# Attention and mixture of experts in one kernel: a GpSimd drain behind the scatters of eight groups, and one weight split of the half group given out two products sooner

## The chip, the core and the metric

The kernel runs on one core of a Trainium2 chip. The metric is the device time of one launch in microseconds (us). The core's engines are TensorE (PE, with its weight loads as PEld), VectorE (DVE), ScalarE (ACT) and GpSimd (POOL); SyncE (SP) issues most DMAs. Each has a queue of its own that it works through in order; engines wait for each other, and for DMAs, by semaphores. GpSimd issues the indirect DMAs (gathers and scatters of rows by an index list).

## The reference

Block-sparse attention, whose output is the input of a mixture of experts with one expert a token:

```python
scores = scale * np.matmul(q, k.transpose(0, 1, 3, 2))   # 4 batches, 8 heads, 768 positions, 64
scores = np.where(mask, scores, -1000000000.0)           # blocks of 32: neighbours, first, last, 3 sampled
attn = np.exp(scores - max); attn /= attn.sum + 1e-9
x = (attn @ v), laid out as 3072 tokens of 512
logits = x @ w_gate + modality_bias[modality_id]         # 8 experts
e_idx = np.argmax(logits, axis=1); gate_w = softmax(logits)[e_idx]
for e in range(8):                                       # w1: 512 x 1024, w2: 1024 x 512
    h = np.maximum(x[mask] @ w1[e], 0.0)
    out[mask] = gate_w[mask, None] * (h @ w2[e])
```

## The kernel before, in words

**Stages.** Attention and routing take about the first half of the launch. The experts follow: tokens are put in groups of 256 that share an expert. Groups 0 and 1 run while attention ends; groups 2 to 11 are the unrolled loop `for g in range(NEAR, NG)` (NEAR is 2, NG 12); what is left over is decided on the chip by two numbers, `total` and `wide`, that every engine loads from `grp` behind the loop. With this input one more group runs, of at most 128 tokens: `half_group(12)`. FIRST_Q is 4.

**A loop group** is `first_layer(g)` (96 matmuls of 256 columns, lines 772 to 774), `relu`, `second_layer(g)` (48 matmuls of 512 columns, lines 787 to 789), and `give(g)`: for each of two halves of 128 rows the sum is copied out of the bank (ACT and DVE, line 792), and GpSimd issues a scatter, an indirect DMA of 128 rows of 2 KB to the output (line 794). Each product is taken with three matmuls, high by high, high by low and low by high parts of the numbers. `split(n)` makes these parts of weight piece n (128 x 1024): ACT casts it (line 723), and DVE, or GpSimd where it is named, subtracts (line 724). `fetch` has SP load the piece.

**Rows in.** `gather_pieces(g + 2)` in `second_layer(g)` has GpSimd issue eight gathers (line 744) into the one buffer `xq`, once `turned_pieces(g + 1)` on DVE (line 751) has read the group before out of it. The last such call is that of group 10, for group 12. So GpSimd's queue in a loop group is: eight gathers, two scatters, the next group's eight gathers.

**The half group** has 24 wide products (lines 946 to 948), two `turn`s (four transposes by PE at line 952, then ACT line 955 and DVE line 956) and 24 products of the second layer, with four weight splits, pieces 4 to 7 of the group. Piece 6 is split by ACT and GpSimd; its low part is read for the first time by the second matmul of `down(g, 4, 0)`.

**What sets the order.** DVE, GpSimd and ACT keep, in the expert stage, the order in which the code is written (`manual_schedule`); PE and SP get theirs from the scheduler. The framework closes the program with lines of its own, shown as L1414 (the last line of the kernel's `with`): waits for all DMAs by SP, then a barrier among all engines with GpSimd drains in it.

Of the kernel before, what the change touches and what calls it, by code (L numbers as in the profile page):

```python
# [31 lines left out]
NG = NTOK // GT  # L32
# [4 lines left out]
FIRST_Q = NEAR + 2  # L37
# [52 lines left out]
def attention_moe(ctx, tc, kD, qD, qH, v0, v1, blocks, modality, w_gate, bias, w1, w2, out):  # L90
    nc = tc.nc
# [29 lines left out]
    with ExitStack() as actx:  # L121
# [582 lines left out]
        def staged(n):  # L704
            return stg[(0, 1, 0, 1, 0, 1, 0, 2)[n] if n < 8 else n % NSTG]
# [15 lines left out]
        def split(n, eng=None):  # L721
            h, l = wh[n % NRING], wl[n % NRING]
            nc.scalar.copy(h, staged(n))  # L723
            (eng or (nc.gpsimd if n in POOL_SPLITS else nc.vector)).tensor_tensor(l, staged(n), h.bitcast(F32), ALU.subtract)  # L724
# [15 lines left out]
        def gather_pieces(g):  # L740
            table = x_d.rearrange("t (r f) -> (t r) f", f=P)
            for t in range(2):
                for k in range(4):
                    nc.gpsimd.indirect_dma_start(  # L744
                        out=xq[0][:, 4 * t + k, :], out_offset=None, in_=table,
                        in_offset=bass.IndirectOffsetOnAxis(ap=gq[:, k, 2 * g + t:2 * g + t + 1], axis=0))

        def turned_pieces(g):
            flat = [xg[2 * (g % 2) + t].rearrange("p (c s) -> p c s", c=4) for t in range(2)]
            for t in range(2):  # L750
                nc.vector.transpose(flat[t].rearrange("p c (k s) -> p k c s", k=4),  # L751
                                    xq[0][:, 4 * t:4 * t + 4, :].rearrange("p k (d c) -> p k c d", c=4))
            for t in range(2):
                h, l = (x[g % 2][:, :, t * P:(t + 1) * P] for x in (xh, xl))
                nc.scalar.copy(h, flat[t])
                nc.vector.tensor_tensor(l, flat[t], h.bitcast(F32), ALU.subtract)

        def column(g, n, xp):
            for c in range(2):
                for t in range(2):  # L760
                    nc.tensor.transpose(xp[:, c * GT + t * P:c * GT + (t + 1) * P],
                                        xg[2 * (g % 2) + t][:, (2 * n + c) * P:(2 * n + c + 1) * P], ident)
            h = xh[g % 2][:, 2 * n:2 * n + 2, :].rearrange("p a b -> p (a b)")
            l = xl[g % 2][:, 2 * n:2 * n + 2, :].rearrange("p a b -> p (a b)")
            nc.scalar.copy(h, xp)
            nc.vector.tensor_tensor(l, xp, h.bitcast(F32), ALU.subtract)
# [15 lines left out]
        def down(g, f, t, o):  # L782
            n = 8 * g + 4 + f // 2
            h, l = wh[n % NRING], wl[n % NRING]
            fs = slice((f % 2) * 512, (f % 2 + 1) * 512)
            ts_ = slice(t * P, (t + 1) * P)
            nc.tensor.matmul(o, lhsT=hh[0][:, f, ts_], rhs=h[:, fs], start=f == 0, stop=False)  # L787
            nc.tensor.matmul(o, lhsT=hh[0][:, f, ts_], rhs=l[:, fs], start=False, stop=False)  # L788
            nc.tensor.matmul(o, lhsT=hl[f // 4][:, f % 4, ts_], rhs=h[:, fs], start=False, stop=f == 7)  # L789

        def give(g, t, o):
            (nc.vector.tensor_copy if t else nc.scalar.copy)(og[t], o)
            ix = si_e[g] if g < NEAR else si[:, 2 * g:2 * g + 2]
            nc.gpsimd.indirect_dma_start(
                out=out_t[t], out_offset=bass.IndirectOffsetOnAxis(ap=ix[:, t:t + 1], axis=0),
                in_=og[t], in_offset=None, bounds_check=NTOK - 1, oob_is_err=False)
# [102 lines left out]
        def ahead(n, *what):  # L899
            for do_, look in what or ((fetch, LOOK_D), (split, LOOK_S)):  # L900
                if n + look < 8 * NGMAX:
                    do_(n + look)
# [19 lines left out]
        def second_layer(g):  # L922
            for k in range(4):
                if k == 0 and FIRST_Q <= g + 1 < NGMAX:
                    turned_pieces(g + 1)
                    if g + 2 <= NG:
                        gather_pieces(g + 2)
                ahead(8 * g + 4 + k)
                for f in (2 * k, 2 * k + 1):
                    for t in range(2):  # L930
                        down(g, f, t, op[t])
                if k == 1 and g + 1 < FIRST_Q:
                    for n in range(2):
                        column(g + 1, n, xp[n])
            for t in range(2):
                give(g, t, op[t])


        def half_group(g):
            hid = xg[2 * ((g + 1) % 2):][:2]  # L940
            x = lambda t, c: t[g % 2][:, c, 0:P]

            def wide_up(k, c):
                h, l = wh[(8 * g + c) % NRING], wl[(8 * g + c) % NRING]
                fs = slice(k * 512, (k + 1) * 512)
                nc.tensor.matmul(hp[k], lhsT=x(xh, c), rhs=h[:, fs], start=c == 0, stop=False)
                nc.tensor.matmul(hp[k], lhsT=x(xl, c), rhs=h[:, fs], start=False, stop=False)
                nc.tensor.matmul(hp[k], lhsT=x(xh, c), rhs=l[:, fs], start=False, stop=c == 3)

            def turn(k):  # L950
                for f in range(4):
                    nc.tensor.transpose(xp[k][:, f * P:(f + 1) * P], hid[k][:, f * P:(f + 1) * P], ident)
                rh = hh[0][:, 4 * k:4 * k + 4, 0:P]
                p_ = xp[k].rearrange("p (f t) -> p f t", f=4)
                nc.scalar.copy(rh, p_)
                nc.vector.tensor_tensor(hl[k][:, :, 0:P], p_, rh.bitcast(F32), ALU.subtract)

            for c in range(2):
                fetch(8 * g + c + LOOK_D)
            for c in range(4):  # L960
                if c == 0:
                    split(8 * g + 4)
                wide_up(0, c)
            nc.scalar.activation(hid[0], hp[0], AF.Relu)
            wide_up(1, 0)
            split(8 * g + 5)
            wide_up(1, 1)
            turn(0)
            wide_up(1, 2)
            wide_up(1, 3)  # L970
            nc.scalar.activation(hid[1], hp[1], AF.Relu)
            split(8 * g + 6, nc.gpsimd)
            for f in range(8):
                if f == 2:
                    turn(1)
                    split(8 * g + 7)
                down(g, f, 0, op[0])
            give(g, 0, op[0])
# [439 lines left out]
```

## Time and profile before

| | |
|---|---|
| median of three runs | 533.4 us (532.72, 533.4, 538.16) |
| the profiled execution's own time | 531.94 us |
| its span, first to last instruction | 530.2 us |
| PE busy | 496.9 us, 94% of the span |
| DVE, ACT, POOL busy | 395.8, 340.7, 295.8 us |
| one loop group, from gather to gather | 21.9 us |

The profile has one profiled execution. Its views are: groups of instructions by line, waits (who waited for whom), the timeline, the chain of work that ended last, and windows (busy time of each engine and DMA traffic in a stretch). A row of one source line lists the sequencer's instructions too (POOLq, SPq: waits, branches, drains), which count as no busy time.

### The profile page before, as it was taken

The page shows a single profiled execution, that of the slowest core. Times are in us where ns is not written, and L with a number is a line of the kernel's source. Part 1 is how long each engine was busy: PE and PEld are TensorE (multiplying, and loading weights), DVE is VectorE, ACT ScalarE, POOL GpSimd, SP SyncE. Part 2 cuts the span into 40 slices and gives each one's busy share as a digit, 9 for nine tenths or more (in the row PEclk, how much of TensorE's full clock was granted, in tenths as well). Part 3 has the DMA queues.
Part 4 walks back from the last instruction along what each step waited for, and adds up shares of the span by engine and source line. Part 5 has one row for each costly group of instructions (what it writes and reads, how often), then busy time and mean ns, then how long its engine had stood idle before and what let it go on. Part 6 is the DMA issues. An engine that isn't in the chain of part 4 may idle for free.

```text
span 530.2 us, 18837 instructions
## 1 busy us (share of the span) xinstructions
PE 496.9 (94%) x7170; PEld 417.9 (79%) x7170; DVE 395.8 (75%) x1137; ACT 340.7 (64%) x777; POOL 295.8 (56%) x507
## 2 busy tenths in 40 slices
PE   7899999999999999799989999999999999999970
PEld 5577776767877777598979898998988989889850
DVE  7995697678689899977975758669586596775830
ACT  3789886979889978845445645547455473654640
POOL 3578674676468875543175527474474754747030
PEclk9999999999999999999999999999999999999995
DMA  7976887868846689757778766685866858768420
GB/s 281 330 226 197 251 243 221 230 209 246 244 148 186 205 227 258 218 190 240 240 282 281 267 204 208 234 291 172 281 224 223 293 161 282 232 214 299 166 85 20
DMA packets 49698, 119.40 MB, mean 225 GB/s; under 512 B 8512, under 2 KB 8896, under 8 KB 49600
## 3 DMA queue, kind: packets, MB, share of 16 engines
q1 hardware_dynamic: 44656, 105.00, 62.6%
q0 software_dynamic: 4944, 13.11, 6.7%
q8 instruction: 58, 0.95, 0.8%
q14 instruction: 40, 0.33, 0.2%
HBM read 105.50 MB, written 12.85 MB: 223 GB/s over the span
## 4 chain that ended last, share of the span: by engine, by line
PE 71%; DVE 10%; DMA 5%; issue 5%; SPq 4%; POOL 2%; ACT 1%; POOLq 0%; DVEq 0%; ACTq 0%
PE bank L789 8%; PE bank L772 8%; PE bank L788 8%; PE bank L787 7%; PE bank L773 7%; PE bank L774 7%; PE bank L535 6%; PE bank L560 5%; PE bank L591 3%; PE bank L582 3%; PE bank L608 2%; DVE slot L724 2%; PE bank L436 2%; DMA slot<-kD 2%; PE bank L598 1%
## 5 line engine op out<-in xcount | busy, mean ns | idle before, releaser
L724 DVE TENSOR_TENSOR slot<-slot 128x1024 fp32r<-128x1024 f32 x96 | 118.7, 1266 | 41.6 <-ACT slot L723 27.2
L744 POOL DMA_INDIRECT slot<-x_d,gq x72 | 94.1, 1307 | 76.2 <-DVE slot L751 56.8
L723 ACT CAST slot<-slot 128x1024 fp32r<-128x1024 f32 x104 | 106.2, 1047 | 39.1 <-PE bank L773 18.6
L772 PE MATMUL bank<-slot 128*128 128x256 f32 x384 | 107.2, 279 | 0.0
L773 PE MATMUL bank<-slot 128*128 128x256 f32 x384 | 106.3, 277 | 0.0
L774 PE MATMUL bank<-slot 128*128 128x256 f32 x384 | 106.3, 277 | 0.0
L551 ACT ACTIVATE a<-y,mn 128x256 f32<-128x256 f32 x176 | 88.7, 512 | 9.9 <-DVE mn L543 8.8
L789 PE MATMUL bank<-slot 128*128 128x512 f32 x200 | 79.0, 395 | 1.6 <-DVE slot L780 1.6
L788 PE MATMUL bank<-slot 128*128 128x512 f32 x200 | 78.6, 393 | 0.6 <-POOL slot L724 0.6
L787 PE MATMUL bank<-slot 128*128 128x512 f32 x200 | 78.3, 391 | 0.0
L773 PEld LDWEIGHTS bank<-slot 128*128 128x128 f32 x384 | 72.3, 188 | 0.4
L772 PEld LDWEIGHTS bank<-slot 128*128 128x128 f32 x384 | 72.1, 188 | 0.6
L774 PEld LDWEIGHTS bank<-slot 128*128 128x128 f32 x384 | 72.1, 188 | 0.0
L543 DVE CUSTOM_DVE_ANT_1 y<-bank,smask 128x256 f32<-128x256 f32 x176 | 66.3, 416 | 1.1 <-PE bank L535 0.7
L483 POOL COPY slot<-slot 128x128 f32 x264 | 65.1, 303 | 0.0
L505 POOL TENSOR_SCALAR slot<-slot 32x1024 f32<-32x1024 f32 x40 | 42.0, 1050 | 24.4 <-issue 10.3
L560 PE MATMUL bank<-ident,a 128*128 128x128 f32 x352 | 52.2, 280 | 2.1 <-DVE mn L543 1.8
L565 ACT COPY at<-bank 128x512 f32<-128x512 f32 x88 | 50.7, 577 | 5.2 <-PE bank L560 5.0
L779 ACT ACTIVATE slot<-bank 128x512 fp32r<-128x512 f32 x48 | 27.2, 598 | 37.9 <-PE bank L774 34.7
L535 PE MATMUL bank<-slot,q_raw 64*32 64x256 f32 x1408 | 49.2, 382 | 1.0 <-DMA q_raw<-qH 0.8
L780 DVE SCALAR_TENSOR_TENSOR slot<-bank,slot 128x512 fp32r<-128x512 f32 x48 | 30.6, 685 | 24.1 <-ACT slot L779 24.1
L789 PEld LDWEIGHTS bank<-slot 128*128 128x128 f32 x200 | 37.6, 188 | 9.8 <-DVE slot L780 2.0
(299 smaller groups left out, 864.2 us busy)
## 6 DMA issues: line engine op xcount, KB each, us to landing
slot<-w SPq DMA_DIRECT2D x105, 512.0 KB
slot<-v SPq DMA_DIRECT2D x180, 128.0 KB
q_raw<-qH SPq DMA_DIRECT2D x22, 256.0 KB
x_d<-xr SPq DMA_DIRECT2D x22, 256.0 KB
slot<-v SPq DMA_DIRECT2D x16, 256.0 KB
slot<-kD SPq DMA_DIRECT2D x13, 256.0 KB
slot<-v SPq DMA_DIRECT2D x4, 768.0 KB
slot<-kD SPq DMA_DIRECT2D x3, 768.0 KB
```

The lines of the kernel that those rows point to most:

```text
L535: nc.tensor.matmul(sp[u][32 * pr:32 * pr + 32, b * 256:(b + 1) * 256], lhsT=q[r, b * NPAIR + pr, n, :], rhs=kv[r, s0:s0 + 8, b, pr, :], st ...
L551: nc.scalar.activation(a[:, u, :], y[:, u, :], AF.Exp, bias=mn[:, u:u + 1], scale=-1.0, accum_out=total[:, u:u + 1])
L560: nc.tensor.transpose(tp[:, k:k + P], a[:, u, c * P:(c + 1) * P], ident)
L723: nc.scalar.copy(h, staged(n))
L724: (eng or (nc.gpsimd if n in POOL_SPLITS else nc.vector)).tensor_tensor(l, staged(n), h.bitcast(F32), ALU.subtract)
L744: nc.gpsimd.indirect_dma_start(out=xq[0][:, 4 * t + k, :], out_offset=None, in_=table, in_offset=bass.IndirectOffsetOnAxis(ap=gq[:, k, 2 * ...
L772: nc.tensor.matmul(o, lhsT=h[:, fs], rhs=xh[g % 2][:, c, :], start=c == 0 and f % 2 == 0, stop=False)
L773: nc.tensor.matmul(o, lhsT=h[:, fs], rhs=xl[g % 2][:, c, :], start=False, stop=False)
L774: nc.tensor.matmul(o, lhsT=l[:, fs], rhs=xh[g % 2][:, c, :], start=False, stop=c == 3 and f % 2 == 1)
L787: nc.tensor.matmul(o, lhsT=hh[0][:, f, ts_], rhs=h[:, fs], start=f == 0, stop=False)
L788: nc.tensor.matmul(o, lhsT=hh[0][:, f, ts_], rhs=l[:, fs], start=False, stop=False)
L789: nc.tensor.matmul(o, lhsT=hl[f // 4][:, f % 4, ts_], rhs=h[:, fs], start=False, stop=f == 7)
```

## The change

A drain is put into GpSimd's queue behind the two scatters of groups 4 to 11, eight in all. In `half_group` the split of piece 6 is written behind `turn(0)`, ahead of the last two wide products and of the second relu, where it stood behind both.

```diff
@@ second_layer
             for t in range(2):
                 give(g, t, op[t])
+            if FIRST_Q <= g < NG:
+                nc.gpsimd.drain()
@@ half_group
             split(8 * g + 5)
             wide_up(1, 1)
             turn(0)
+            split(8 * g + 6, nc.gpsimd)
             wide_up(1, 2)
             wide_up(1, 3)
             nc.scalar.activation(hid[1], hp[1], AF.Relu)
-            split(8 * g + 6, nc.gpsimd)
             for f in range(8):
```

ACT's rows of the half group, before: L955 are the two turns, L971 is the second relu, L723 are the casts of pieces 4, 5, 6 and 7, L792 the copy out.

```order
L723 CAST slot<-slot 128x1024
L964 ACTIVATE slot<-bank 128x512
L723 CAST slot<-slot 128x1024
L955 CAST slot<-bank 128x4x128
L971 ACTIVATE slot<-bank 128x512
L723 CAST slot<-slot 128x1024
L955 CAST slot<-bank 128x4x128
L723 CAST slot<-slot 128x1024
L792 COPY slot<-bank 128x512
```

The same stretch of ACT's queue with the change; lines behind the drain's stand two or three higher.

```order
L723 CAST slot<-slot 128x1024
L966 ACTIVATE slot<-bank 128x512
L723 CAST slot<-slot 128x1024
L957 CAST slot<-bank 128x4x128
L723 CAST slot<-slot 128x1024
L974 ACTIVATE slot<-bank 128x512
L957 CAST slot<-bank 128x4x128
L723 CAST slot<-slot 128x1024
L792 COPY slot<-bank 128x512
```

The cast of piece 6 has changed places with the second relu. PE's, DVE's and SP's rows are in the same order as before.

GpSimd's rows at the end of the loop, with the change: the scatters of groups 10 and 11 (L794), the two loads of `grp`, the branches, and the subtraction of piece 6 (L724). Drains are not printed; one stands behind each pair of scatters.

```order
L794 DMA out<-slot,si 3072x512 [waits DMASW4_49,Activation_49]
L794 DMA out<-slot,si 3072x512 [waits DMASW5_49,DVE_49]
L794 DMA out<-slot,si 3072x512 [waits DMASW6_49,DMASW4_49,Activation_49]
L794 DMA out<-slot,si 3072x512 [waits DMASW7_49,DMASW5_49,DVE_49]
L1367 TENSOR_LOAD grp [waits DVE_49]
L1368 TENSOR_LOAD grp
L1373 COMPARE_AND_BRANCH
L1375 COMPARE_AND_BRANCH
L724 TENSOR_TENSOR slot<-slot 128x1024 [waits DMAHW0_49,DMAHW5_49,PE_49,Activation_49]
```

No printed row of GpSimd has moved; the drain of group 11 stands between the fourth row and the fifth, so the loads, the branches and the subtraction are now behind it.

## Rows read from the trace of the kernel before

**Rows 1.** The page's first line.
```profile
span 530.2 us, 18837 instructions
```
**Rows 2.** Waits of PE, 270 us to the end: total, times, longest (us).
```profile
PE bank L789 <- DVE slot L780: 1.6, 1, 1.6
PE bank L788 <- POOL slot L724: 0.6, 1, 0.6
```
**Rows 3.** The chain that ended last, its last piece: start, us, what.
```profile
515.77 0.99 POOL out L794
```
**Rows 4.** Windows of the tail: length, busy us by engine, PE clock, DMA share, GB/s.
```profile
517.00:519.00 2.00, 0.00 (x0) 0.00 (x0) 0.00 (x0) 0.00 (x0) 0.00 (x0) 0.52 0.34 123
519.00:520.00 1.00, 0.00 (x0) 0.00 (x0) 0.00 (x0) 0.00 (x0) 0.00 (x0) 0.50 0.03 8
521.00:530.20 9.20, 0.00 (x0) 0.00 (x0) 0.00 (x0) 0.00 (x0) 0.00 (x0) 0.50 0.00 1
```
**Rows 5.** GpSimd's drains by line (end, start): ns min/median/max, first and last start.
```profile
L1414 POOLq DRAIN  x3: 45/107/8705, 520.6 to 529.9; - x3
L1411 POOLq DRAIN  x1: 171/171/171, 0.4 to 0.4; - x1
```
**Rows 6.** Waits of SP, 510 us to the end.
```profile
SPq L1414 <- PEq L1414: 10.0, 2, 9.5
```
**Rows 7.** GpSimd's indirect DMAs by line: count, busy us, mean ns, idle before.
```profile
L744 POOL DMA_INDIRECT slot<-x_d,gq x72 | 94.1, 1307 | 76.2 <-DVE slot L751 56.8 <-issue 19.4
L794 POOL DMA_INDIRECT out<-slot,si x21 | 23.0, 1094 | 26.5 <-ACT slot L792 21.0 <-issue 5.5
...
L729 POOL DMA_INDIRECT slot<-x_d,gi x4 | 4.6, 1150 | 7.4 <-DVE gi L987 6.5 <-issue 0.6 <-DMA slot<-w 0.3
L729 POOL DMA_INDIRECT slot<-x_d,gi_e x4 | 4.5, 1116 | 0.9 <-issue 0.6 <-POOL slot L505 0.2 <-POOL slot L724 0.2
L794 POOL DMA_INDIRECT out<-slot,si_e x4 | 4.2, 1060 | 10.9 <-ACT slot L792 10.1 <-DVE gend L1121 0.5 <-issue 0.3
```
**Rows 8.** Timeline of GpSimd, one loop group's end: start, us, what, idle before.
```profile
441.07 1.03 POOL L744 DMA_INDIRECT slot<-x_d,gq  x1 [0.30 <-issue]
...
443.71 1.17 POOL L794 DMA_INDIRECT out<-slot,si  x1 [0.30 <-issue]
451.31 0.99 POOL L744 DMA_INDIRECT slot<-x_d,gq  x1 [6.43 <-DVE slot L751]
```
**Rows 9.** Windows ahead of two groups' gathers, columns as in rows 4.
```profile
450.00:451.00 1.00, 1.00 (x6) 0.81 (x5) 1.00 (x3) 0.00 (x0) 0.00 (x0) 1.00 0.00 0
...
472.00:473.00 1.00, 1.00 (x6) 0.83 (x5) 1.00 (x2) 0.04 (x1) 0.00 (x0) 1.00 0.01 4
```
**Rows 10.** Timeline of DVE in the same loop group.
```profile
449.96 2.06 DVE L751 STREAM_TRANSPOSE slot<-slot 128x512 f32<-128x512 f32 x2
```
**Rows 11.** Timelines of ACT, GpSimd and PE about the half group.
```profile
503.47 0.98 POOL L794 DMA_INDIRECT out<-slot,si  x1 [0.30 <-issue]
506.58 0.59 ACT L955 CAST slot<-bank 128x512 fp32r<-128x512 f32 x1 [0.27 <-PE bank L952]
508.46 1.04 ACT L723 CAST slot<-slot 128x1024 fp32r<-128x1024 f32 x1
509.59 2.39 POOL L724 TENSOR_TENSOR slot<-slot 128x1024 fp32r<-128x1024 f32 x1 [5.14 <-ACT slot L723]
512.03 0.50 PE L788 MATMUL bank<-slot 128*128 128x512 f32 x1 [0.55 <-POOL slot L724]
```
**Rows 12.** Window behind group 11's scatters, columns as in rows 4.
```profile
508.00:508.50 0.50, 0.50 (x3) 0.28 (x2) 0.17 (x1) 0.50 (x2) 0.00 (x0) 1.00 0.00 0
```
**Rows 13.** GpSimd's first load of grp and its branches, by line.
```profile
L1365 POOLq TENSOR_LOAD <-grp x1: 289/289/289, 502.8 to 502.8; - x1
...
L1373 POOLq COMPARE_BRANCH  x2: 34/38/41, 503.5 to 518.1; - x2
```

## The prediction, made before the changed kernel ran

> **What bounds the kernel now.** I read the waits of PE first, since PE is busy 94% of the span. From 270 us to its last matmul PE is stopped twice, by 1.6 and 0.6 us [rows 2]: the expert stage is PE's own work, and nothing that the change does there can gain more than these few tenths. Then I read where the chain that ended last stops. Its last piece is GpSimd's scatter of the half group, 515.77 to 516.76 us [rows 3], but the span is 530.2 us [rows 1]. So 13.4 us, 2.5% of the span, lie behind the last instruction that any engine counts as busy. The windows of this tail show what is in it: the scatter's 256 KB move between 517 and 519 (123 GB/s times 2 us), 8 GB/s are left in the next microsecond, and from 521 on nothing moves [rows 4]. Nine microseconds hold neither work nor data. The rows of the closing line name them: GpSimd's drains there are three, the first starts at 520.6 us and the longest takes 8705 ns; since the last starts at 529.9, the long one can only be the first, 520.6 to 529.3 [rows 5]. SP waits out the barrier for 9.5 us in the same place; the view names PE's sequencer, which is merely one of those that wait with it [rows 6].
>
> **What the long drain does.** All data has landed before it starts, so it does not wait for a transfer. Its two successors take 107 and 45 ns, and the one at the program's start, ahead of any DMA, 171 ns [rows 5]. What sets it apart is what GpSimd has issued since the drain before it: 72 + 21 + 4 + 4 + 4 = 105 indirect DMAs [rows 7]. My reading is that a drain goes through the indirect DMAs issued since the last drain and settles each: 8705 / 105 = 83 ns for each, an estimate. That the next drain takes 107 ns says that a DMA once settled is not gone through again.
>
> **The eight drains, term by term.** At the drain of group 4, 42 DMAs are open (8 gathers of whole rows, 24 of pieces, 10 scatters), 3.5 us at 83 ns; at those of groups 5 to 10 ten each, 0.8 us; at group 11 two; at the end of the program one, the half group's scatter. 42 + 60 + 2 + 1 = 105: the work is the same and changes place. The end's drain is then bounded below by the bare 45 ns and above by the 171 ns of the first drain plus one DMA's 83 ns; I take 0.15 us. **Term 1: 8.70 - 0.15 = 8.55 us gained.**
>
> What hides the others: a drain has also to wait until its group's scatters have landed. In the loop group shown the second scatter is handed over from 443.71 to 444.88, and GpSimd then stands idle 6.43 us until DVE's transposes release the next gather at 451.31 [rows 8]. From 450.0 to 451.0 no DMA at all is in flight [rows 9], so the scatters have landed within 5.1 us of 444.88. Group 9 is the tightest: 4 GB/s from 472 to 473 [rows 9], and its next gather stands at 473.2 in the same rhythm of 21.9 us. Six of the eight drains (groups 4 to 9) have this gap of 6.43 us; the settling of the gathers falls into the landing time. Even 3.5 us of settling for group 4, begun as soon as its scatter is handed over, end inside it. Behind the drain stand only the next gathers, and if they start late there is cover still: a gather handed over at 441.07 lands, if it takes no longer than the scatter (6.3 us from its start), by 447.4, and DVE reads it at 449.96 [rows 8, 10]: 2.6 us. If that cover goes too, DVE's transposes are late, and behind them the casts of the next group's rows. **Term 2: 0 us**, as long as a drain ends less than 9.0 us (6.43 + 2.6) after its scatter. Group 10's drain has no gather behind it and is free.
>
> **The drain of group 11 and the moved split** share a term. Now ACT's cast of piece 6 runs 508.46 to 509.50 behind the second relu, GpSimd subtracts from 509.59 for 2.39 us, and PE stands 0.55 us for the result [rows 11]; this is one of the two stops. With the split ahead of the relu, the cast can follow the turn's cast, which ends at 507.17 [rows 11], and ends at about 508.2; the relu behind it is some 0.2 us later, and its first reader, the second turn's transposes, stands behind six products of PE, so that costs nothing. By the cast alone GpSimd could subtract at 508.3 and the whole 0.55 us would be gained. But the drain of group 11 stands ahead. The scatters are handed over by 504.45 [rows 11] and have landed by 508.0, since from there to 508.5 no DMA moves [rows 12]. Then GpSimd has to load two numbers and pass two branches, which took it from 502.8 to 503.6 [rows 13], some 0.9 us with the gaps. So the subtraction starts between 509.0 and 509.4, and 0.2 to 0.55 us are gained. **Term 3: 0.35 us gained.** The point from which it turns: a drain that ends after 508.7 makes PE wait longer than before, one microsecond for each.
>
> [...]
>
> **The sum.** 8.55 + 0 + 0.35 = 8.9 us, made against the profiled execution's 531.94 us, which is 1.5 us below the median of the three timed runs. The four executions together (531.94, 532.72, 533.4, 538.16) have their middle at 533.06; 533.06 - 8.9 = **524.2 us**.
>
> **The rivals.**
> *A: the tail stays.* The 8.7 us are no settling of earlier DMAs but something of the closing line that the first drain there meets. Then the inner drains are as cheap as the bare ones and the end keeps its 8.7 us: 533.06 - 0.35 = 532.7 us. For it: no row before shows a second drain behind DMAs. Against it: the same kind of drain takes 107 ns in the same line.
> [...]
>
> *B, on the other side: each drain behind a DMA costs 8.7 us, whatever is open.* The place is GpSimd's queue. From the first gather to the end of the second scatter it needs 15.5 us of a group's 21.9 (451.31 less 21.9, to 444.88); with 8.7 more 24.2, so each of six groups is 2.3 us longer, 13.6 us less the cover of 2.6: 11 us. Group 11's drain ends at 513.2, the subtraction starts at 514.1 in place of 509.6, and PE stands 4.5 us longer. The end keeps its drain: 533.06 + 15.5 = 548.6 us. It decides from 6.43 + 2.6 = 9.0 us a drain, counted from the scatter, on. Against it: the 107 and 45 ns, if those are drains of the same kind.
>
> *C: settling is slow behind a landing.* If the drain of group 11 ends 3 us after its scatters have landed, term 3 turns to a loss of 2.6 us: 533.06 - 8.55 + 2.6 = 527.1 us. Against it: nothing but the arithmetic of 83 ns.
>
> If the 8.7 us are a cost of the first drain behind DMAs alone, that of group 4 pays it: 2.3 us beyond its gap, within the cover of 2.6, and the time is that of the forecast.
>
> **How the numbers follow.** The forecast, with the first-time variant, 0.82; A 0.08; B 0.05; C 0.05. The forecast's own range is 531.94 - 9.1 (8.66 with the bare drain, and 0.45) = 522.8 to 533.4 - 8.4 (the dearest last drain, and nothing in term 3) = 525.0. Stretched over C, and a little down for a series of runs that is as a whole lower, it is 522.3 to 527.5; A and B lie outside. A measurement of this kernel tells about 1% from no change, 5.3 us: the forecast and C are faster by more (0.87), A is the same (0.08), B slower (0.05).
>
> **What the profile of the changed kernel would show.** Right, if: the longest drain of the closing line takes under 0.3 us and the span ends about 5 us behind the last scatter; eight new drains stand at line 938, that of group 4 no shorter than the others and all of them ended before the next gather, whose idle time is still put down to DVE's transposes; PE's stop at the half group's second product of piece 6 is between 0 and 0.35 us. Wrong, if: the last drain is still several microseconds (A); the idle time ahead of the gathers is no longer DVE's, the loop group is longer than 21.9 us, and PE has stops in the loop (B); or PE stands more than 0.55 us for GpSimd's subtraction (C). The weakest step is the reading of 8705 ns as 105 times 83, since it rests on one long drain.

## The result, and the profile after

The changed kernel takes 528.56 us (median of six runs, 525.72 to 536.48) where the kernel before, in the same series, takes 537.06 (six runs, 532.72 to 538.91). The ratio is 0.986 with the interval 0.982 to 0.990: 1.4% faster, where the forecast was 8.9 us, 1.7%. The time itself lies 1.1 us above the forecast's range. One of the six runs was disturbed and is left out of the ratio.

| from the two profiled executions, us | before | after | difference | forecast |
|---|---|---|---|---|
| first instruction to group 2's first product | 281.89 | 281.47 | -0.4 | |
| groups 2 to 11, first product to first wide product | 219.93 | 223.47 | **+3.5** | 0 |
| half group, first wide product to start of the last scatter | 13.95 | 13.45 | -0.5 | -0.35 |
| end of the last scatter's hand-over to the end of the span | 13.43 | 4.6 | **-8.8** | -8.55 |
| span | 530.2 | 524.0 | -6.2 | -8.9 |

The first products are read from PE's timeline, here of the changed kernel (start, us, what); before they start at 281.89 and 501.82.

```profile
281.47 0.39 PE L772 MATMUL bank<-slot 128*128 128x256 f32 x1
...
504.94 0.39 PE L948 MATMUL bank<-slot 128*128 128x512 f32 x1
```

Two terms came as said. The third, "the inner drains cost nothing", did not: 3.5 us came back in the loop. GpSimd's drains of the changed kernel by line (ns min/median/max, first and last start; compare [rows 5]):

```profile
L938 POOLq DRAIN  x8: 4992/13188/14724, 349.1 to 506.1; - x8
...
L1416 POOLq DRAIN  x3: 57/107/1358, 521.2 to 523.7; - x3
```

The 8705 ns are gone from the closing line. The drains in the loop look long because the trace has them start before the scatters ahead of them have run (group 4's at 349.08, its scatters at 354.41 and 355.73); what counts is when they end. The tail by windows (columns as in [rows 4]):

```profile
519.40:521.40 2.00, 0.00 (x0) 0.00 (x0) 0.00 (x0) 0.00 (x0) 0.00 (x0) 1.00 0.35 127
521.40:523.00 1.60, 0.00 (x0) 0.00 (x0) 0.00 (x0) 0.00 (x0) 0.00 (x0) 0.62 0.02 5
523.00:524.00 1.00, 0.00 (x0) 0.00 (x0) 0.00 (x0) 0.00 (x0) 0.00 (x0) 0.50 0.00 0
```

The scatter's 256 KB move until 521.4, and the closing drain, begun at 521.2, ends at 522.6: its 1.36 us are mostly the landing, since the last update of that scatter's semaphore stands at 522.52. The drain is 7.35 us shorter, and it begins 1.86 us behind the scatter's hand-over in place of 3.88. The prediction did not look at what stands between the two: an instruction in GpSimd's sequencer row, begun 0.02 us behind the scatter's start in both traces, that is shorter too, before and after:

```profile
L1373 POOLq INC_SWDGE_SEM  x1: 2275/2275/2275, 515.8 to 515.8; - x1
```

```profile
L1375 POOLq INC_SWDGE_SEM  x1: 194/194/194, 518.4 to 518.4; - x1
```

The closing drain begins 2.6 us behind its end in both. Over all runs it takes 2.28 us with 105 indirect DMAs open (the kernel before), 2.18 with 100 (one_scatter), 1.44 with 63 (drain4_only), 0.24 with three (drain10) and 0.19 with one (the changed kernel): about 20 ns for each.

The half group's rows answer to [rows 11], ACT's cast of piece 6 and GpSimd's subtraction:

```profile
510.18 1.05 ACT L723 CAST slot<-slot 128x1024 fp32r<-128x1024 f32 x1
...
512.20 2.39 POOL L724 TENSOR_TENSOR slot<-slot 128x1024 fp32r<-128x1024 f32 x1 [4.63 <-ACT slot L974]
```

The drain of group 11 (506.1 plus 4.99) ends at 511.1, inside the cast, and the subtraction begins 0.97 us behind the cast. PE's waits from 270 us on (compare [rows 2]; the 1.6 us stop there falls ahead of 270 in this execution) show no stop for that subtraction any more, and a new one:

```profile
PE bank L787 <- ACT slot L779: 0.4, 1, 0.4
```

PE waits 0.4 us for ACT's relu. It is the start of the loss. GpSimd's and ACT's timelines lead back from it (start, us, what, idle before):

```profile
364.59 0.98 POOL L744 DMA_INDIRECT slot<-x_d,gq  x1 [7.71 <-DVE slot L756]
...
377.55 1.22 POOL L794 DMA_INDIRECT out<-slot,si  x1 [0.31 <-issue]
379.08 1.00 POOL L794 DMA_INDIRECT out<-slot,si  x1 [0.30 <-issue]
...
380.84 2.06 ACT L779 ACTIVATE slot<-bank 128x512 fp32r<-128x512 f32 x4 [4.20 <-PE bank L774]
```

The gather of group 7 begins after 7.71 us of idle time in place of 6.43 [rows 8], so 1.28 us late. The view names DVE, because a drain counts as no busy instruction: the drain of group 4 (349.1 plus 14.7) ends at 363.8, and each gather that waits for a drain in these traces begins 0.81 us behind its end (in this one 364.59 behind 363.79, and 476.26 behind 475.46). Gathers and scatters follow each other at 0.30 us, with nothing to wait for, so group 5's scatters are 1.28 us late too. Behind them ACT's four relus of group 6, which should start 0.68 us apart as PE finishes the banks, start late and run back to back. In the kernel before, the same place:

```profile
378.03 1.16 POOL L794 DMA_INDIRECT out<-slot,si  x1 [0.30 <-issue]
...
379.91 2.25 ACT L779 ACTIVATE slot<-bank 128x512 fp32r<-128x512 f32 x4 [2.85 <-PE bank L774]
```

In both, the first relu starts 0.7 to 0.8 us behind the end of the second scatter, though the product it waits for was done before. With the scatter late the relu is late, and PE stops. That PE's notice is late, and not ACT, is shown by PE's semaphore, whose updates the trace keeps: the four stand at 380.82, 380.90, 380.97 and 381.12 us, for products that end (by the profile's model) at 379.07, 379.75, 380.43 and 381.11. After the stop PE's first layers take 11.47 us instead of 11.07. That is seen in the mean of the 256-column products from 400 to 480 us (line, tile, shape, count, busy us, mean ns), before:

```profile
L772 PE MATMUL bank<-slot 128*128 128x256 f32 x107 | 29.6, 276 | 0.0
```

and after, with PE busy all the time in both:

```profile
L772 PE MATMUL bank<-slot 128*128 128x256 f32 x108 | 30.3, 281 | 0.0
```

Each of the five first layers behind the stop is 0.40 us longer, 2.0 us of the 3.5. The rest is the stop, by which group 6's second layer starts 0.54 us late, a short second one of 0.14 us ahead of group 11's second layer, and these two second layers, 0.38 us longer each. The second stop has the same cause: group 9's drain ended at 475.5, 7.6 us with the 0.81 until the gather against a gap of 6.43, and the relu behind group 10's scatters starts 1.45 us behind its product. The granted clock is 1.00 over the whole loop in both.

### The profile page after: what moved, and what is told of

Same layout as the page of the kernel before. It is cut to its first block, busy times and chain, and to the rows that moved or that the text cites. A ratio compares the mean times of both kernels' runs of the same rounds, so it can differ in the third digit from the quotient of the medians.

```text
span 524.0 us, 18845 instructions
## 1 busy us (share of the span) xinstructions
PE 500.3 (95%) x7170; PEld 421.1 (80%) x7170; DVE 396.8 (76%) x1137; ACT 340.5 (65%) x777; POOL 296.7 (57%) x507
## 4 chain that ended last, share of the span: by engine, by line
PE 72%; DVE 14%; issue 5%; DMA 3%; ACT 2%; SPq 1%; POOL 1%; POOLq 0%; DVEq 0%; ACTq 0%
PE bank L789 8%; PE bank L772 8%; PE bank L787 8%; PE bank L788 8%; PE bank L774 8%; PE bank L773 8%; PE bank L535 6%; PE bank L560 5%; PE bank L582 3%; PE bank L591 3%; DVE y L543 2%; DMA slot<-kD 2%; DVE slot L724 2%; PE bank L608 2%; PE bank L598 1%
## 5 line engine op out<-in xcount | busy, mean ns | idle before, releaser
L724 DVE TENSOR_TENSOR slot<-slot 128x1024 fp32r<-128x1024 f32 x96 | 118.4, 1262 | 42.2 <-ACT slot L723 22.6
L723 ACT CAST slot<-slot 128x1024 fp32r<-128x1024 f32 x104 | 106.1, 1047 | 40.1 <-PE bank L773 26.1
```

## The experiments

In all tables below "loop" is the stretch from group 2's first product to the first wide product (219.93 us before), "half" and "tail" are the third and fourth rows of the table above. "Held" says whether the first relus behind the scatters of groups 3 and 4 start 0.3 to 0.4 us behind their products or within 0.1 us. The expectations number relus by the group whose scatters stand ahead of them: "the first relu of group 5" and "group 5's second layer" are, in the code's count, those of group 6, and so on. A series is what ran together on one chip.

### What a drain costs

`drains_only`: the eight drains, the split not moved.

> The eight drains without the moved split. By settling (each indirect DMA since the last drain costs its share once): the closing line's first drain takes under 1.5 us, most of it the last scatter's landing, and the span ends about 5 us behind the last scatter, as in the changed kernel. The drain of group 4 ends some 1.7 us after its last scatter has landed, against 0.45 us for the others, so group 7's gathers and group 5's scatters are about 1.2 us late; if that lateness is what made the second relu of group 5's hidden layer late, PE stops about 0.5 us ahead of group 5's second layer again and runs its 256-column matmuls at 118 ns in place of 113 from there. If the slow rhythm is chance, it stands at another place or nowhere. In the half group GpSimd's subtraction waits for the later cast, so PE stops about 0.55 us: 0.5 us slower than the changed kernel at equal rhythm.

`split_only`: the split moved, no drains.

> The moved split without any drain. By the prediction's own steps: the closing line's first drain keeps its 8.7 us and the span ends 13.4 us behind the last scatter; GpSimd subtracts right behind the cast, which is some 1.4 us earlier against PE's products, and PE's stop of 0.55 us in the half group goes: 0.5 us faster than before, which timing cannot tell from no change. Nothing holds GpSimd in the loop, so by the theory that late scatters start the slow rhythm PE's first layers stay at 11.07 us each; by chance they may be 11.47.

`drain10`: the split moved, one drain behind group 10.

```diff
-            if FIRST_Q <= g < NG:
+            if g == NG - 2:
                 nc.gpsimd.drain()
```

> One drain alone, behind the scatters of group 10, where GpSimd stands idle 13.5 us, and the moved split. By settling: 102 DMAs are open there; it ends about 4.2 us (41 ns each, the part that comes behind the landing) after the scatters have landed, near 498 us, well ahead of group 11's scatter. Three DMAs are left for the closing line's first drain, so the tail is as short as with eight drains. No gather of the loop has a drain ahead of it, so no scatter is late and PE's first layers keep 11.07 us each: 8.8 (tail) + 0.5 (half group) less than before, about 522.6 us beside 531.9, and 3 us faster than the changed kernel. If the drain costs a fixed 8 us or so whatever is open, it still fits the gap, and the time is the same; if the slow rhythm is chance, the time scatters as that of the changed kernel does.

`drain4_only`: one drain, behind group 4, the split not moved (`if g == FIRST_Q`).

> One drain alone, behind the scatters of group 4, without the moved split. By settling, 42 of the 105 DMAs are settled there and 63 are left: the closing line's first drain takes 63 x 83 ns = 5.2 us. If the long drain is a cost of the first drain behind DMAs only, it takes under 0.3 us; if it belongs to the closing line, 8.7 us. Group 7's gathers are about 1.2 us late, and with them group 5's scatters; by the theory that this starts PE's slow rhythm, PE stops ahead of group 5's second layer.

| kernel | time | ratio, interval | loop | half | tail | longest closing drain |
|---|---|---|---|---|---|---|
| drains_only | 527.23 | 0.986, 0.982 to 0.989 | 220.87 | 15.15 | 5.0 | 1.85 |
| split_only | 533.45 | 0.998, 0.996 to 1.000 | 219.92 | 13.32 | 13.6 | 8.71 |
| drain10 | 523.13 | 0.980, 0.977 to 0.984 | 220.36 | 13.29 | 5.0 | 1.83 |
| drain4_only | 530.19 (one run) | | 222.96 | 13.96 | 9.65 | 5.26 |

The profiled execution of split_only took 543.32 us and reached group 2's first product only at 293.7; only its stretches from there on are used. The closing line of drain4_only:

```profile
L1416 POOLq DRAIN  x3: 57/107/5262, 522.3 to 528.2; - x3
```

63 indirect DMAs are issued behind group 4's drain: 5262 / 63 = 83.5 ns each, as 8705 / 105 = 82.9. A run further down with 100 takes 8297, 83.0 each. So the closing drain takes its 83 ns for every indirect DMA issued since the last drain, at 63, 100 and 105 of them; rival A and the first-time variant are out.

In the loop the same work does not hide under the landing. Behind the last landing of its scatters the drain of group 4 still takes 1.76 us, with 42 DMAs open; those of groups 5 to 10 take 0.45 us with ten; that of drain10 4.22 us with 102. That is 41 to 45 ns for each open DMA, after the data has arrived. The windows of the changed kernel show it for group 4:

```profile
362.00:363.00 1.00, 1.00 (x6) 0.81 (x5) 1.00 (x3) 0.00 (x0) 0.00 (x0) 1.00 0.00 0
```

The last landing stands at 362.02, no DMA moves from 362.0 to 363.0, and the drain ends at 363.79. In drain10 the 4.22 us fall where GpSimd has nothing to do:

```profile
L938 POOLq DRAIN  x1: 17099/17099/17099, 481.0 to 481.0; - x1
```

```profile
487.62 1.16 POOL L794 DMA_INDIRECT out<-slot,si  x1 [0.31 <-issue]
...
502.32 0.97 POOL L794 DMA_INDIRECT out<-slot,si  x1 [13.53 <-ACT slot L792]
```

It ends at 498.1, 4.2 us ahead of the next scatter, which still waits for ACT. PE has no stop in the loop; its 0.4 us over 219.93 is one first layer of 11.57, group 2's, ahead of any change.

split_only shows what the moved split is worth: its half group is 0.6 us shorter than before. drains_only shows what the drain of group 11 can cost. Its half group is 1.2 us longer than before, and 1.7 longer than in the changed kernel. Its row of GpSimd's subtraction and PE's waits from 500 us on:

```profile
513.61 2.35 POOL L724 TENSOR_TENSOR slot<-slot 128x1024 fp32r<-128x1024 f32 x1 [6.37 <-ACT slot L957]
```

```profile
PE bank L788 <- POOL slot L724: 1.7, 1, 1.7
```

Its drain of group 11 ended at 512.5, because the scatters ahead of it landed 5.1 us after their hand-over, not 3.6; the subtraction followed 1.1 us later. ACT's cast, though not moved, was done at 512.3, ahead of the drain's end, so the moved split would have changed nothing here, and the expected cause, the later cast, was not it. This is rival C's place, though not its cause: the drain itself is short there (0.12 us behind the landing), the landing is late. In its loop PE has the same stop of 0.4 us behind group 5's scatters, but the first layers behind it keep 11.07 us, so the eight drains cost 0.9 us there and not 3.5.

### What stops PE

The theory: PE's notices of finished products are held back until about 0.7 us behind the second scatter. Four small GpSimd copies make the scatters of group 5 late without a drain (`late4`; `late8` has eight):

```diff
+            if g == 5:
+                for _ in range(4):
+                    nc.gpsimd.tensor_copy(smask.rearrange("p a b -> p (a b)")[:, 0:P], ident)
             for t in range(2):
                 give(g, t, op[t])
```

> The kernel before, without any drain, with four small copies by GpSimd between group 5's gathers and its scatters, so that these two scatters alone are some 1.2 to 1.6 us late. If PE's completion signals are held until about 0.7 us after the second scatter has been handed over, the first relu of group 5 starts 0.7 us behind that hand-over, some 1 to 1.4 us later than in the kernel before, and PE stops about 0.5 us ahead of group 5's second layer, though there is no drain; the rhythm of its first layers behind the stop is 11.07 or 11.47 us. If it was the drain that held the signals, the relu starts as before and PE does not stop.

> The same with eight copies, the scatters 2.4 to 3 us late. If the signals are held by the hand-over of a scatter alone, the first relus start in time, before the second scatter, or are held by the first one: at most about as long as one scatter takes to be handed over (1.2 us) and 0.7 us more, counted from the scatter that is being handed over when bank 0 is done. If the drain held them, nothing is late. The stop, if there is one, shows a second draw of the rhythm behind it.

`one_scatter` leaves the second scatter of groups 5 to 9 out; `after_again` is the changed kernel.

> The kernel before with the second scatter of groups 5 to 9 left out (half of these groups' output rows are not written). If the second scatter's hand-over holds PE's signals, the first relu of these groups starts 0.04 us behind the end of bank 0's last matmul in place of 0.36 to 0.42, and that of groups 3, 4 and 10 as before. If the gathers or the first scatter hold them as well, it does not change. PE's time stays, since the relu is ahead of need; the closing line's first drain has five DMAs less, 0.4 us.

> The changed kernel once more. By late scatters: the drain of group 4 ends about 1.7 us behind the landing, group 5's scatters are late and PE stops ahead of group 5's second layer, as in the first profile; the rhythm behind it is 11.47 us or 11.07, and the time differs by 0.4 us for each group at the slow one, up to 3 us. If the first profile's stop was chance, there is none here.

| kernel | held | time | ratio, interval | loop | half | tail |
|---|---|---|---|---|---|---|
| late4 | no | 534.7 | | 219.92 | 13.94 | 13.7 |
| late8 | no | 533.82 | | 219.93 | 13.94 | 13.6 |
| one_scatter | no | 535.5 | | 219.92 | 13.94 | 13.1 |
| after_again | no | 523.7 | 0.979, 0.974 to 0.983 | 219.93 | 13.30 | 3.5 |

These four ran as a series on another chip than the first four, and there nothing is held in any of them. The changed kernel has the same late gather as before and loses nothing by it:

```profile
369.47 0.98 POOL L744 DMA_INDIRECT slot<-x_d,gq  x1 [7.73 <-DVE slot L756]
...
383.94 1.00 POOL L794 DMA_INDIRECT out<-slot,si  x1 [0.30 <-issue]
...
383.96 1.96 ACT L779 ACTIVATE slot<-bank 128x512 fp32r<-128x512 f32 x3 [2.46 <-PE bank L774]
```

The relu starts while the second scatter is still being handed over. So the late gather alone costs nothing, as term 2 had it; and late4 and one_scatter had tested nothing. I ran them again, with the changed kernel and drain10 side by side.

> The kernel before with four small GpSimd copies ahead of group 5's two scatters, so that these are handed over about 1 us late, with no drain anywhere. Theory S (the notices of PE's finished products are held back until about 0.7 us behind the hand-over of the second scatter): the first relu of group 5 starts 0.65 to 0.8 us behind the second scatter's end and so 1 us late, PE stops 0.3 us or more for it, though there is no drain. Rival D (it is the drain that holds them): the relu starts at its usual place, no stop. Rival K (the holding is there in some launches or on some chips only): in this launch all relus of groups 3 to 10 start within 0.1 us of the product that they wait for, and no stop comes. End drain 8.7 us, the time that of before.

> The kernel before without the second scatter of groups 5 to 9: rows 128 to 255 of these five groups are not written to the output, all else is as before. Theory S: where notices are held at all, the first relu of groups 6 to 10 comes about 1.3 us sooner relative to its product than that of the other groups, since the last scatter is over 1.3 us sooner. Rival K: no relu is held in this launch, none moves. The end drain takes 8.3 us, 100 indirect DMAs at 83 ns.

> The changed kernel again, beside drain10_b on the same chip. The drain behind group 4 ends 1.7 to 1.8 us behind the last landing (42 DMAs at 41 ns). Theory S, if notices are held in this launch: a stop of PE of 0.3 us or more ahead of group 5's second layer, first layers from then on either 11.07 or 11.47 us each, ratio 0.983 to 0.990. Rival K, if none is held: no stop, all first layers 11.07 us, ratio 0.977 to 0.982. Half group 13.3 to 13.5 us, tail 3.5 to 5 us in both.

> One drain behind the scatters of group 10 alone, with the moved split. Both theories: no stop in the loop, all first layers 11.07 us, the drain some 17 us long and 4.2 us behind the last landing (102 DMAs at 41 ns), half group 13.3 us, tail 3.5 to 5 us, ratio 0.977 to 0.983. Against the changed kernel: 2 to 4 us faster where notices are held, level within 0.5 us where they aren't.

| kernel | held | time | ratio, interval | loop | half | tail |
|---|---|---|---|---|---|---|
| late4_b | yes | 534.46 | | 219.92 | 13.95 | 13.4 |
| one_scatter_b | yes | 532.51 | | 219.93 | 13.96 | 13.0 |
| after_b | yes | 530.07 | 0.990, 0.980 to 1.000 | 224.13 | 14.19 | 4.9 |
| drain10_b | yes | 525.17 | 0.985, 0.978 to 0.992 | 219.93 | 13.30 | 4.6 |

This time notices were held; it is the chip of the first four experiments. after_b has the stop behind group 5's scatters and a second, short one (0.16 us) behind group 10's, which are late because group 9's drain ended late (477.8); the loop is 4.2 us longer than that of drain10_b, of which 0.4 is group 2's first layer, ahead of any drain. Their medians are 4.9 apart. But late4_b contradicts my theory as I had put it:

```profile
381.91 1.02 POOL L794 DMA_INDIRECT out<-slot,si  x1 [0.55 <-issue]
383.24 1.00 POOL L794 DMA_INDIRECT out<-slot,si  x1 [0.30 <-issue]
```

```profile
382.05 2.64 ACT L779 ACTIVATE slot<-bank 128x512 fp32r<-128x512 f32 x4 [2.46 <-PE bank L774]
```

All four relus run in their own rhythm (2.64 us for four) while two scatters are handed over in the middle of them. Late scatters as such hold nothing there. one_scatter_b doesn't tell: its relus are in time, but its single scatter is over 1.75 us before they are due. What late4_b has that the changed kernel has not is a pause of 3 us in GpSimd's row of indirect DMAs: eight gathers, a pause, two scatters, in place of ten in a row.

The last pair therefore separates three things. `late_gathers` makes the ten late, in a row, without any drain. `after_pause` is the changed kernel, with its drain and its late gather, and a pause of two copies ahead of group 5's scatters, made as in late4. The edit of late_gathers:

```diff
+                    if g + 2 == 7:
+                        for _ in range(2):
+                            nc.gpsimd.tensor_copy(xq[0][:, 0, :], ident)
                     if g + 2 <= NG:
                         gather_pieces(g + 2)
```

> The kernel before with two small GpSimd copies into the gather buffer ahead of group 7's gathers: these gathers and the scatters of group 5 behind them stay ten in a row, 1.2 to 1.6 us late, with no drain in the loop. Theory L (the lateness of the ten is enough, the drain itself does nothing): the first relu of group 5 starts 1.4 to 2.1 us behind the product that it waits for, about 0.75 us behind the second scatter's end, and PE stops 0.3 to 0.7 us for it, in a launch in which the relus of groups 3 and 4 start 0.3 to 0.4 us late; in a launch where those start within 0.1 us, nothing is held. Rival D (it takes a drain): the relu starts within 0.45 us of its product and PE does not stop. End drain 8.7 us, the time that of before, or up to 3 us more by L.

> The changed kernel with two small GpSimd copies between group 7's gathers and group 5's scatters: the drain behind group 4 ends late as before it did, the gathers are late, the scatters 1.4 us later still. Theory Q (the notices are held only behind ten indirect DMAs in a row, and a pause in the row lets them pass): the relus of group 5 start within 0.1 us of their products, no stop of PE at group 5, the first layers behind it 11.07 us; a later drain that ends late may still make a stop at group 10. Rival L2 (late scatters hold the notices, pause or not): the relu of group 5 starts about 0.75 us behind the second scatter's end, 3 us late, and PE stops 1.5 to 2 us. In a launch where nothing is held in groups 3 and 4 the run tells nothing.

They were run three times, since nothing was held in the first two series.

> The same kernel as late_gathers in another launch: the ten indirect DMAs of group 7's gathers and group 5's scatters 1.2 to 1.6 us late without a drain in the loop. Theory L (the lateness is enough): where the relus of groups 3 and 4 start 0.3 to 0.4 us late, that of group 5 starts 1.4 to 2.1 us behind its product and PE stops 0.3 to 0.7 us. Rival D (it takes a drain): no stop, the relu within 0.45 us. Where nothing is held in groups 3 and 4: nothing at group 5 either, as in the launch before.

> The same kernel as after_pause in another launch: the changed kernel with a pause of two small copies ahead of group 5's scatters. Theory Q (only ten in a row hold the notices): where the relus of groups 3 and 4 start 0.3 to 0.4 us late, that of group 5 starts within 0.1 us of its product, no stop at group 5. Rival L2 (late scatters hold them, pause or not): that relu 3 us late, a stop of 1.5 to 2 us. Where nothing is held in groups 3 and 4: no stop, and 3 us faster than the launches of the changed kernel that had one.

> late_gathers once more, in a third launch, for one in which the relus of groups 3 and 4 start late. Theory L: then the relu of group 5 starts 1.4 to 2.1 us behind its product and PE stops 0.3 to 0.7 us without any drain. Rival D: no stop. Where nothing is held in groups 3 and 4: no stop, loop as in the kernel before.

> after_pause once more, in a third launch. Theory Q: where the relus of groups 3 and 4 start late, that of group 5 starts within 0.1 us of its product and PE does not stop there. Rival L2: that relu 3 us late, a stop of 1.5 to 2 us. Where nothing is held: no stop, time 521 to 526 us.

| series | held | late_gathers: time, loop | after_pause: time, loop |
|---|---|---|---|
| first | no | 538.3, 219.93 | 525.34, 219.92 |
| second | no | 534.26, 219.92 | 521.36, 220.35 |
| third | yes | 536.7, **222.95** | 524.68, 220.93 |

late_gathers_c has no drain in the loop and has the stop, with the late relu behind it and PE's waits from 270 us on:

```profile
381.15 1.00 POOL L794 DMA_INDIRECT out<-slot,si  x1 [0.30 <-issue]
...
382.92 2.07 ACT L779 ACTIVATE slot<-bank 128x512 fp32r<-128x512 f32 x4 [4.21 <-PE bank L774]
```

```profile
PE bank L789 <- DVE slot L780: 1.6, 1, 1.6
PE bank L788 <- POOL slot L724: 0.5, 1, 0.5
PE bank L787 <- ACT slot L779: 0.4, 1, 0.4
```

Its loop is 3.0 us longer than before, with the slow rhythm behind the stop (281 ns again). So no drain is needed; the lateness of the ten is enough. after_pause_c, on the same chip, has the drain, a gather as late as in the changed kernel and scatters later still, and the relus behind group 5's scatters run in time:

```profile
380.74 1.02 POOL L794 DMA_INDIRECT out<-slot,si  x1 [0.56 <-issue]
382.06 1.00 POOL L794 DMA_INDIRECT out<-slot,si  x1 [0.30 <-issue]
...
380.78 2.64 ACT L779 ACTIVATE slot<-bank 128x512 fp32r<-128x512 f32 x4 [2.46 <-PE bank L774]
```

Its one stop in the loop (0.5 us) is behind group 10's scatters, where no pause was put: group 9's scatters landed late there and their drain ended at 474.7. With this the chain to the stop is shown, as far as single executions go: a drain that ends late makes ten indirect DMAs in a row late; in four of the seven series PE's notices wait until 0.5 to 0.8 us behind such a row; moved late enough, that wait reaches PE. What in the chip holds the notices, and why only in some series, is not settled, nor why a row of ten holds them and the last two of it behind a pause do not. Nor is it shown why the slow rhythm follows most of these stops and not that of drains_only.

One rival is untested: that the profile's own recording holds the notices. The traces differ by series in what they keep, whatever the kernel: 8890 to 9004 semaphore updates in each of the twelve with held notices, 10031 to 10132 in each of the eight without. No run here tells whether the notices would be held in an execution that is not recorded.

## Why the prediction was right and where it failed

**Term 1, the end (8.55 us): right.** The tail lost 8.8 us in the profiled pair. The reading of 8705 ns as 105 times 83, called the weakest step, holds at 63 and at 100 DMAs as well. The last drain was mis-sized (0.15 forecast, 0.19 to 1.85 measured), because it can start before the last scatter has landed (521.24 against 522.52 in the first profile) and then contains the landing; that time was in the tail before, too, ahead of the drain. So the 8.8 are 7.35 us of the drain and 2.0 of its sooner start, less 0.5 behind it: the sum came out as forecast by two parts of which the prediction knew one. GpSimd's first drain in the closing line took 8.7, 8.3, 5.3 and below 1.9 us with 105, 100, 63 and at most three DMAs open.

**Term 3, the half group (0.35 us): right, where the landing was soon enough.** 0.5 us were gained in the profiled pair, 0.65 in after_again and drain10_b. The turning point was named (a drain of group 11 that ends too late), but its likelihood was judged from one landing of 3.6 us. It was 3.4 in the profiled run, 4.2 in after_b, which lost 0.24 us in place of a gain, and 5.1 in drains_only, which lost 1.2. The half group follows that drain one to one: it ends 6.12, 6.89 and 7.86 us behind the first wide product in these three, and the half group takes 13.45, 14.19 and 15.15. From the drain's end to the subtraction it is 1.13 us, not the 0.9 of the prediction, so the turning point lies some 0.2 us sooner. No landing of group 11's scatters was less than 2.99 us behind the hand-over here, and the last scatter of the program, alone, took 1.7 to 3.7.

**Term 2, the inner drains (0 us): this step failed**, in two places.
The first is "the settling of the gathers falls into the landing time. Even 3.5 us of settling for group 4 ... end inside it". Half of it does not: 41 to 45 ns a DMA came behind the last landing, with landings from 3.8 to 6.3 us behind the hand-over. The sum was to be 5.1 us of landing, plus 1.76, plus 0.81 until GpSimd's next DMA: 7.7 us against a gap of 6.43. This is 1.3 us over, within the 9.0 us that the prediction set as its limit. Group 9, called the tightest, overran too: its scatters landed 6.3 us behind the hand-over, where the prediction had gone by the 5.1 us of another group.
The second is that limit. Its cover of 2.6 us was read from the gathers' readers on DVE, and DVE was indeed never late. But behind the gathers stand the next scatters, which nobody waits for. The prediction has "Behind the drain stand only the next gathers"; where PE's notices are held they carry the lateness to ACT's relus, then to PE. The trace before shows the sign of it, a first relu that idles 2.85 us and takes 2.25 us for four where 0.68 us apart would make 2.64, and I did not ask what it waited for.

**The size of the miss.** Where nothing is held, the late drains cost the loop nothing, as term 2 had it: after_again has the loop of before to 0.01 us and the ratio 0.979, 11.3 us of 535.3, with an interval that just reaches the forecast's 8.9. Where it is held, 0.9 us (drains_only) to 3.8 us (after_b, without group 2's 0.4) are lost in the loop. The time lies 4.4 us above the forecast's 524.2, and of this 4.0 are the base: the sum was made from four executions with their middle at 533.06, and the six of the whole series had theirs at 537.06. The medians' difference, 8.5 us, is but 0.4 short of 8.9, while the profiled pair differs by 6.2; how many of the six executions lost 3.5 us in the loop no trace tells. So the base alone is enough to put the time outside the range, and term 2 is what was wrong about the kernel: with the base of 533.06 the same difference would have made 524.6, and the forecast would have been met by luck. In the traces kept, the stretch ahead of the loop makes the scatter of the base, not the change: group 2's first product starts between 280.9 and 288.0 us (split_only's apart), while the loop without a stop repeats to 0.01 us but for a first layer that now and then takes 0.4 more. The range should have been that of the base, some 4 us to each side, or the forecast a difference alone.

**The rivals.** A fell by drain4_only's 63 times 83.5 ns; B by the same, and no drain cost 8.7 us in the loop. Two of B's signs came all the same, a stop of PE and a longer loop; the third, idle time ahead of the gathers that is no longer DVE's, the view cannot give, since it counts no drain. C was right about the direction of the risk and wrong about its mechanism: time behind a landing is real, but it is short with two DMAs open (0.12 us) and long with 42 (1.76 us), so it struck at group 4 and not at group 11.

**The better version.** One drain behind group 10, with the split moved, has 102 of 105 DMAs settled in 13.5 us in which GpSimd has nothing to issue. It took 523.13 and 525.17 us in two series (ratios 0.980 and 0.985), both on chip 0, where notices were held. Beside the changed kernel in one series it was 4.9 us faster by the medians, and in the profiled executions its loop is 4.2 us (3.8 without group 2's first layer) and its half group 0.9 us shorter. The two ratios' intervals still overlap, and one of the changed kernel's four runs, 523.27, is faster than all four of drain10_b. Where nothing is held, the changed kernel's 0.979 is level with it.

## What to carry to other kernels

In these runs a GpSimd drain paid for every indirect DMA issued since the drain before it: 83 ns each at the program's end, and in the loop 41 to 45 ns each behind the last landing. So put one where GpSimd has nothing to issue for longer than that, as in the 13.5 us behind group 10 here, and count what was issued ahead of it. When a step on a queue becomes late, follow every instruction behind it on that queue, also those that no one waits for, and judge the cover from each.

## What the runs showed of the hardware that was not expected

All figures are of this case's traces, with the run beside them.

- GpSimd's drain: 83 ns for each open indirect DMA where all, or all but the last, had landed before it started (8705 ns for 105 in the kernel before, 8297 for 100 in one_scatter, 5262 for 63 in drain4_only). Where it started earlier, 41 to 45 ns each behind the last landing (0.45 us for ten and 1.76 for 42 in the changed kernel, 4.22 for 102 in drain10).
- INC_SWDGE_SEM, which the traces show in GpSimd's sequencer row, begun with the last scatter: 194 ns with one indirect DMA open (the changed kernel), 2275 ns with 105 (the kernel before), so about 20 ns for each.
- In four of the seven series, in all their kernels, ACT's first relu behind ten indirect DMAs in a row started no sooner than 0.47 to 0.83 us behind the last one's hand-over (0.65 to 0.72 in the kernel before, 0.48 to 0.76 in the changed one), even where its product was done 1.8 us before (379.07 against a relu at 380.84 in the changed kernel); in the other three it was never more than 0.04 us behind its product. It went with the series, not with the kernel: the experiments on chips 0 (both series) and 15 have it, those on chips 1, 10 and 12 do not. Whether the recording has a part in it is open.
- PE took two times for the same 96 products of 256 columns, 11.07 us in the kernel before and 11.47 behind the changed kernel's stop (276 and 281 ns a product by the view), at a granted clock of 1.00 in both. Behind a stop of 0.4 us the slower one held for the rest of the loop in the first profile, after_b, drain4_only and late_gathers_c, and not in drains_only. Group 2's first layer was also 0.4 us longer in drain10, after_b and after_pause_b, with no such stop ahead of it.
